# Own rows of the keys first, no zero fills and a new listed order, in a sparse attention with an MLP behind it

## The chip, the cores and the metric

One core of a Trainium2 chip runs the kernel. The metric is the device time of one execution in microseconds; the figure shown is the median of three runs. The profile is of one such execution, and its span runs from the first to the last instruction. The engines are TensorE (PE, with PEld for its weight loads), VectorE (DVE), ScalarE (ACT), GpSimd (POOL) and SyncE (SP). In this kernel POOL issues all loads from DRAM and SP all stores but one.

## The reference

Block-sparse attention for 4 batches, 8 heads, 768 positions and 64 dimensions, then an MLP of 512 to 2048 to 512 over the 3072 tokens. Each query sees the keys at a distance under 16, and the 24 blocks of 32 keys by the block's maximum (with log 32 added to the score) and the block's mean value.

```python
k_sum = k.reshape(B, H, nb, block, D).max(axis=3)
v_sum = v.reshape(B, H, nb, block, D).mean(axis=3)
scores_l = scale * np.matmul(q, k.transpose(0, 1, 3, 2))
mask_l = np.abs(pos[:, None] - pos[None, :]) < window
scores_s = scale * np.einsum('bhsd,bhnd->bhsn', q, k_sum)
scores_s = scores_s + np.log(block)
scores_l_m = np.where(mask_l, scores_l, -1000000000.0)
scores_all = np.concatenate([scores_l_m, scores_s], axis=-1)
...
a = np.exp(scores_all)
a = a / (np.sum(a, axis=-1, keepdims=True) + 1e-09)
v_all = np.concatenate([v, v_sum], axis=2)
return np.matmul(a, v_all).astype(np.float32)
...
h = x @ w_in
relu6 = np.clip(h + 3.0, 0.0, 6.0)
g = h * relu6 / 6.0
return (g @ w_out).astype(np.float32)
```

## The kernel before

**Tiling.** The 768 positions of a batch are cut into 12 tiles of 64 keys. A tile's window has 96 key rows: 64 own and 32 of a neighbour. Behind them stand 24 rows for the blocks, 120 rows in all (`KEYS`). The 64 queries of tile t are shifted by 16 against its keys, so that the window covers every key at a distance under 16. `kaug[p]` holds the keys of head pair p by tile, as columns; `vaug[b % 2]` holds the values with the 120 rows on partitions, and with a column of ones whose product is the softmax's denominator. Before the change a window is previous 32 rows, then own 64: own rows lie in rows 32 to 95, and queries are shifted down by 16. The first tile wraps around to the last rows of the batch.

**Steps of one batch.** Keys are transposed (`k_step` for batch 0, by products with the unit matrix `ident`; `turn` for the others, by VectorE), the block maximum is taken (kmax) and spread over the tiles. Values land by a strided load, which turns f32 into bf16, into the own rows; the neighbour's 32 rows are copied from the own rows of another tile (`halo`, batches 0 and 1) or loaded again (`load_ahead`, batches 2 and 3). Block sums of V are products with the indicator `ind` (`vsum_first`, `vsum`), spread over tiles by copies. Scores go to PSUM, ScalarE takes the exp, VectorE masks, values are a product with `vaug`, VectorE normalizes, and the result is transposed into `x`. A batch has two halves of 384 positions; each half is a tile s of the MLP (8 in all). `f1` multiplies by `w_in` (16 items of 128 features, 4 products of 384 columns each), with relu on ScalarE and the gate on VectorE; `f2` multiplies by `w_out` (three row groups ts, four parts of four products), copies to SBUF and stores.

**Order.** Every step registers operations with a key. The string `ORDER` lists all keys in the order in which they are issued; each engine works its own operations strictly in that order, and `:A` or `:D` picks ScalarE or VectorE for a copy. Keys: `c` constants; `K`, `Q`, `V`, `H` loads of keys, queries, values and neighbour values; `Q0w2` a wide load of queries; `I` and `O` loads of `w_in` and `w_out`; `k`, `q`, `w` transposes of K and Q; `h` halos; `u` block sums; `s` scores; `v` values; `F` and `G` the two MLP products. So `K00` loads pair 0 of batch 0 (192 KB), `K02` pairs 2 and 3 (384 KB); `c.1` makes `ident` and `c.2` the band of the mask, both on POOL. `u0` sums V of pairs 0 and 1, `v410` and `v411` are the values of batch 0's second half.

A token `~n`, `-n`, `_n` or `=n` places **fill products** on the tile `idle`, whose results nobody reads: n of 512, n of 128, n of 64 columns, or one of 64 n columns (`keep`, line 774).

PSUM has three buffers h, one o and two pairs S. Each F item takes an h (some early ones may take an S) and frees it with its gate.

**Zero fills.** `c.8` to `c.15` (`empty`, line 280) write zeros to the 32 neighbour rows of `vaug` ahead of the halos, so that the sums over 96 rows read defined data; five stand on ScalarE and three on VectorE.

**The end.** The last G group (s = 7, ts = 1) is done in column pieces of 256, 128 and 128, each with its own copy; the middle 128 are copied and stored by ScalarE (line 698), the others are stored by SP (lines 694 and 695, two DMAs where rows wrap).

Of the kernel before, what the change touches and what calls it, by code (L numbers as in the profile page):

```python
# [15 lines left out]
D = 64  # L16
# [17 lines left out]
s020.1 v01.3 v00.3 V03.0 u1.0 u1.3:A h030.0:D s030.0 k3.4 ~2 s030.1 u1.4:D v01.4 h031.0:D Q0w0.0 Q0w1.0 v01.5:D Q0w2.0 =1 q3.0
q3.1:D q2.0 u1.1:A u1.2:D s020.2 v02.0 v02.1 v02.2 s021.0 v02.3 s030.2 v03.0 v03.1 q2.1:A v03.2 s011.0 v03.3 v00.4 v00.5:D
v02.4 s021.1 s011.1 s021.2 v03.4 v03.5:D s011.2 v02.5:A s031.0 s031.1 s001.0 s031.2 I2.0 F0x3.0 F0x3.1 F0x3.2 F0x3.3 F0x3.4
F0x3.5 I4.0 F0x6.0 F0x6.1 F0x6.2 F0x4.0 F0x4.1 F0x4.2 F0x4.3 v411.0 v411.1 F0x5.0 F0x4.4 F0x4.5 v411.2 s001.1 I8.0 u0.2:A
s001.2 F0x8.0 F0x8.1 F0x8.2 F0x5.1 I0.0 F0x5.2 F0x11.0 F0x1.0 F0x11.1 F0x11.2 F0x1.1 F0x1.2 F0x1.3 F0x1.4 F0x1.5 v410.0 v410.1
F0x7.0 F0x7.1 F0x7.2 v410.2 F0x10.0 F0x10.1 I12.0 F0x13.0 F0x13.1 F0x15.0 F0x15.1 F0x13.2 F0x10.2 v411.3 v411.4:D v410.3
v410.4:A F0x15.2 F0x14.0 F0x14.1 F0x14.2 F0x9.0 F0x9.1 F0x9.2 F0x0.0 F0x0.1 F0x2.0 F0x2.1 K13.0 K10.0 c.12:A F0x0.2 K12.0 K11.0  # L40
w10.0 Q1w1.0 F1x14.0 F1x14.1 F1x14.2 F1x4.0 F1x4.1 F1x4.2 F1x2.0 F1x2.1 F1x2.2 w10.1:D F0x2.2 F0x2.3 F0x2.4 F0x12.0 F0x12.1
F0x12.2 F1x8.0 F1x8.1 F1x8.2 F1x1.0 F1x1.1 F1x1.2 F0x0.3 F0x0.4 F0x0.5 F0x2.5 F1x9.0 F1x9.1 F1x9.2 F1x5.0 F1x5.1 F1x5.2 F1x15.0
F1x15.1 w11.0 w11.2 F1x15.2 w11.3:D Q1w4.0 Q1w2.0 Q1w0.0 w10.2 w10.3:D q6.0 q6.1:A q7.0 q7.1:A F1x7.0 F1x7.1 w11.1:A F1x7.2
F1x12.0 F1x12.1 F1x12.2 O0.0 G02x0.0 Q1w5.0 Q1w3.0 q4.0 q4.1:A q5.0 q5.1:A F1x6.0 F1x6.1 F1x6.2 O1.0 G02x0.1 s100.0 s100.1
s100.3 F1x3.0 w12.0 F1x11.0 F1x11.1 w13.0 w13.2 F1x3.1 F1x11.2 w12.2 w12.1:D O2.0 G02x0.2 s101.0 s101.1 O3.0 F1x10.0 G02x0.3
G02x0.4:A w13.3:D w13.1:A s101.3 F1x0.0 G00x0.0 G00x0.1 w12.3:D s100.2 s101.2 s100.4 V10.0 h100.0:D F1x10.1 h110.0:A F1x10.2
F1x3.2 s110.0 s110.1 s110.2 s101.4 s110.3 G00x0.2 G00x0.3 G00x0.4:A V12.0 u4.0 h130.0:D h120.0:A F1x0.1 u4.1:D u4.2:A u4.4:D
u4.3:D u4.5:D G02x0.5 G01x0.0 G01x0.1 G01x0.2 s110.4 F1x0.2 h111.0:A v100.0 v100.1 v100.2 h121.0:A v101.0 v101.1 v101.2 G01x0.3
G01x0.4:A K20.0 K21.0 K22.0 K30.0 K23.0 w21.0 F1x13.0 F1x13.1 F1x13.2 v100.3 v100.4:A w20.0 w21.3 G12x0.0 w21.2:A v101.3
v101.4:A V22.0 H2.0 h101.0:A w20.3 G12x0.1 G12x0.2 F2x2.0 F2x2.1 F2x11.0 F2x2.2 F2x11.1 F2x11.2 s111.0 w23.0 s111.3 F2x1.0  # L50
F2x1.1 F2x1.2 F2x3.0 F2x3.1 F2x3.2 F2x15.0 F2x15.1 F2x15.2 Q22.0 w23.3 G12x0.3 s111.1 G12x0.4:A F2x5.0 F2x5.1 h131.0:A F2x5.2
F2x6.0 G10x0.0 s111.2 w22.0 w22.3 s111.4 w23.4:A V20.0 H2.1:A K33.0 F2x13.0 F2x13.1 F2x13.2 G10x0.1 F2x6.1 F2x0.0 F2x0.1 F2x0.2
u5.0 u5.1:A u5.5:A F2x6.2 v110.0 v111.0 v111.1 v111.2 Q30.0 F2x4.0 F2x4.1 F2x4.2 Q21.0 Q23.0 Q20.0 w22.4:A F2x10.0 F2x10.1
# [24 lines left out]
F6x3.2 G52x0.3 G52x0.4:D F6x5.0 F6x5.1 F6x11.2 F6x2.0 F6x2.1 F6x5.2 F6x2.2 G51x0.0 F6x13.0 F6x13.1 F6x6.0 F6x15.0 G51x0.1
v311.6 F6x6.1 F6x6.2 F6x15.1 v311.5 v311.4 F7x5.0 F6x15.2 F6x13.2 F7x5.1 F7x5.2 F7x13.0 F7x9.0 F7x13.1 F7x13.2 F7x9.1 F7x9.2
G51x0.2 F7x12.0 F7x12.1 F7x12.2 F7x10.0 F7x10.1 F7x10.2 F7x1.0 G51x0.3 F7x1.1 F7x1.2 G51x0.4:A F7x3.0 G40x0.5 F7x6.0 F7x6.1  # L80
F7x6.2 G51x0.5 F7x8.0 F7x8.1 F7x8.2 G62x0.0 F7x4.0 F7x4.1 F7x4.2 F7x3.1 F7x3.2 F7x2.0 G62x0.1 F7x15.0 F7x2.1 F7x2.2 F7x15.1
F7x15.2 F7x0.0 G62x0.2 F7x0.1 G62x0.3 F7x7.0 F7x7.1 F7x0.2 G71x0.0 G62x0.4:D G62x0.5 F7x7.2 F7x11.0 F7x11.1 G61x0.0 F7x11.2
F7x14.0 G71x0.1 G71x0.2 G71x256.0 G61x0.1 F7x14.1 F7x14.2 G71x0.3 G71x0.4:A G72x0.0 G72x0.1 G71x0.5 G41x0.5 G70x0.0 G61x0.2
# [79 lines left out]
def kernel(  # L163
# [80 lines left out]
    def low(x):  # L244

        return (1 - x) * HQ
# [17 lines left out]
    def spread_mask():  # L264
        nc.vector.tensor_copy(mask[:], band[:].unsqueeze(1).to_broadcast([WIN, NQ, QB]))
        nc.vector.memset(mask[0:BLK, 0, PAD:QB], 0.0)
        for lo in (BLK, 2 * BLK):
            nc.vector.memset(mask[lo:lo + BLK, 0, 0:PAD], 0.0)
# [48 lines left out]
    def load_wide(b, u):  # L317
# [492 lines left out]
```

## Time and profile before

| what | us |
|---|---|
| median of 3 runs (216.97 to 217.23) | 217.14 |
| span of the profiled execution | 214.9 |
| TensorE busy | 208.8 |
| VectorE busy | 162.7 |
| ScalarE busy | 135.9 |
| F products (line 667, 500 on h) | 91.1 |
| G products (line 684, 336 on o) | 81.7 |
| fill products (line 778), 80 of them | 9.5 |

Busy time counts the union of an engine's instructions, and ends of products are modelled. A row of a timeline gives start, duration, engine, line, operation, output and input, and, in brackets, how long the engine was idle before and what ended that. A row of a group gives count, busy time, mean in ns and idle time before. A row of DMA issues gives queue, count, size and the time from issue to landing. The DMA engines are nearly always busy in the first 91 us, since loads run far ahead of their use.

### The profile page before, as it was taken

How to read it: one execution, taken by the hardware profiler on the slowest of the kernel's cores; microseconds unless marked ns; L12 is line 12 of the kernel's file. 1: busy time of each engine (PE TensorE's matmuls, PEld its weight loads, DVE VectorE, ACT ScalarE, POOL GpSimd, SP SyncE). 2: the span in 40 equal slices, each digit the busy share in tenths (PEclk: the TensorE clock that was granted, in tenths of full speed). 3: DMA queues.
4: the chain of work that ended last, by engine and by line, in shares of the span. 5: the costliest groups of instructions: out<-in, count | busy, mean ns of one | idle time of the engine just before them, and what ended most of it. 6: DMA issues, size and time to landing. Idle time of an engine off the chain costs nothing.

```text
span 214.9 us, 6125 instructions
## 1 busy us (share of the span) xinstructions
PE 208.8 (97%) x2564; PEld 119.7 (56%) x2564; DVE 162.7 (76%) x318; ACT 135.9 (63%) x264; POOL 49.5 (23%) x66
## 2 busy tenths in 40 slices
PE   7998999999999999999999999999999999999994
PEld 7566656555555565565555555555555555564443
DVE  6987999999899999898899889887865555550021
ACT  3987878887898988756578696566346355520110
POOL 7977358906643244000000000000000000000000
PEclk9999999999999999999999999999999999999999
DMA  5999999999999999930334234113314400113123
GB/s 75 159 155 189 203 188 170 190 203 162 206 160 187 181 135 151 108 146 11 38 37 143 28 37 110 49 21 39 70 19 81 78 0 3 49 49 122 52 80 139
DMA packets 91724, 22.68 MB, mean 106 GB/s; under 512 B 82224, under 2 KB 88752, under 8 KB 91696
## 3 DMA queue, kind: packets, MB, share of 16 engines
q0 software_dynamic: 62288, 14.41, 72.7%
q1 hardware_dynamic: 29264, 7.80, 15.4%
q8 instruction: 20, 0.33, 0.6%
q10 hardware_dynamic: 144, 0.07, 0.1%
q14 instruction: 8, 0.07, 0.1%
HBM read 28.82 MB, written 6.29 MB: 163 GB/s over the span
## 4 chain that ended last, share of the span: by engine, by line
PE 86%; POOL 5%; DMA 4%; DVE 1%; ACT 1%; issue 1%; POOLq 0%
PE h L667 38%; PE o L684 33%; PE h L684 5%; DMA qwide<-in_q_dram 4%; PE S L624 3%; PE S L513 3%; POOL vaug L344 2%; PE S L554 1%; ACT vaug L242 1%; POOL first L306 1%; PE S L637 1%; POOL qwide L326 1%; PE S L440 1%; PE S L667 1%; POOL first L313 1%; PE h L582 1%
## 5 line engine op out<-in xcount | busy, mean ns | idle before, releaser
L667 PE MATMUL h<-x,win 128*128 128x384 bf16 x500 | 91.1, 326 | 0.3 <-DVE g L672 0.3
L671 ACT ACTIVATE r<-h 128x384 f32<-128x384 f32 x125 | 58.7, 492 | 38.8 <-PE h L667 36.8
L672 DVE SCALAR_TENSOR_TENSOR g<-r,h 128x384 bf16<-128x384 f32 x125 | 65.7, 546 | 22.7 <-ACT r L671 20.1
L684 PE MATMUL o<-wout,g 128*128 128x512 bf16 x336 | 81.7, 379 | 0.0
L667 PEld LDWEIGHTS <-win 128*128 128x128 bf16 x512 | 48.7, 98 | 35.9 <-issue 0.5
L684 PEld LDWEIGHTS <-g 128*128 128x128 bf16 x416 | 38.7, 98 | 37.4 <-issue 0.3
L521 ACT ACTIVATE at<-S 120x768 bf16<-120x768 f32 x24 | 18.6, 811 | 5.5 <-PE S L513 5.4
L242 ACT COPY ot<-o 128x512 f32<-128x512 f32 x17 | 10.0, 586 | 15.4 <-PE o L684 14.2
L522 DVE TENSOR_TENSOR at<-at,mask 96x768 bf16<-96x768 bf16 x24 | 12.6, 549 | 2.0 <-ACT at L521 1.6
L606 DVE TENSOR_TENSOR xn<-S,rc 128x768 bf16<-128x768 f32 x14 | 13.3, 950 | 0.3
L242 DVE COPY ot<-h 128x512 f32<-128x512 f32 (+1 forms) x3 | 1.6, 555 | 14.3 <-PE h L684 14.3
L344 POOL DMA_DIRECT2D vaug<-in_v_dram x10 | 11.8, 1191 | 0.4 <-DMA first<-in_k_dram 0.2
L684 PE MATMUL h<-wout,g 128*128 128x128 bf16 (+2 forms) x80 | 11.4, 294 | 0.0
L468 DVE TENSOR_REDUCE red<-kaug 128x24 bf16<-128x768 bf16 x12 | 11.2, 942 | 0.1
L242 ACT COPY vaug<-vaug 32x640 bf16<-32x640 bf16 (+3 forms) x17 | 8.9, 574 | 0.8 <-DMA vaug<-in_v_dram 0.5
L242 ACT COPY vaug<-vs 24x1536 bf16<-24x1536 bf16 x6 | 8.8, 1468 | 0.6 <-DVE vs L242 0.5
L456 DVE STREAM_TRANSPOSE kaug<-kraw 128x768 bf16<-128x768 bf16 x8 | 8.1, 1020 | 0.3 <-PE S L513 0.3
L778 PE MATMUL o<-idle 128*128 128x64 bf16 (+2 forms) x70 | 7.0, 278 | 1.1 <-DVE idle L288 1.1
L334 POOL DMA_DIRECT2D kraw<-in_k_dram x8 | 5.9, 737 | 8.9 <-DVE kaug L456 7.3
L513 PEld LDWEIGHTS <-kaug 32*128 32x128 bf16 x576 | 5.3, 92 | 4.4 <-issue 3.6
L643 DVE STREAM_TRANSPOSE y<-xn 128x768 bf16<-128x768 bf16 x8 | 7.6, 964 | 0.2
L624 PEld LDWEIGHTS <-at 120*64 120x64 bf16 x336 | 6.2, 111 | 2.6 <-issue 1.5
(107 smaller groups left out, 183.6 us busy)
## 6 DMA issues: line engine op xcount, KB each, us to landing
out_dram<-ot SPq DMA_DIRECT2D x19, 256.0 KB, 2.3
vaug<-in_v_dram POOLq DMA_DIRECT2D x6, 384.0 KB, 13.1
wout<-in_moe_w_out_dram POOLq DMA_DIRECT2D x4, 512.0 KB, 9.9
win<-in_moe_w_in_dram POOLq DMA_DIRECT2D x3, 512.0 KB, 10.8
kraw<-in_k_dram POOLq DMA_DIRECT2D x8, 192.0 KB, 12.9
x<-y SPq DMA_DIRECT2D x64, 24.0 KB, 2.0
first<-in_k_dram POOLq DMA_DIRECT2D x6, 192.0 KB, 12.3
first<-in_q_dram POOLq DMA_DIRECT2D x6, 192.0 KB, 12.3
```

Of the source, the lines that this page charges most:

```text
L242: {"ACT": nc.scalar.copy, "DVE": nc.vector.tensor_copy, "POOL": nc.gpsimd.tensor_copy}[eng](o, i)
L344: op("POOL", "dma128", lambda: nc.gpsimd.dma_start(out=o[BLK:WIN, a:z, 0:D], in_=rows[:, a:z]), w=[("v", b % 2, c) for c in range(lo, hi)] ...
L468: op("DVE", "max", lambda: nc.vector.tensor_reduce(red.slot[:], w[:, :, BLK:WIN].rearrange("p t (n c) -> p t n c", n=2), axis=AX.X, op=ALU ...
L513: nc.tensor.matmul(X[g // 2].slot[:, g % 2, i * QB:(i + 1) * QB], kaug[2 * u + m][rows, t], qT[rows, 2 * u + m, t * QB:(t + 1) * QB], star ...
L521: op("ACT", "exp", lambda a=a, e=e: nc.scalar.activation(a, X[e].slot[0:KEYS, :, 0:HALF], AF.Exp, scale=scl), r=[X[e]], w=[("at", p, half)])
L522: op("DVE", "masking", lambda m=m: nc.vector.tensor_tensor(m, m, mask[:, low(half):low(half) + HQ].unsqueeze(1).to_broadcast([WIN, 2, HQ, ...
L606: nc.vector.tensor_tensor(o, src[..., 0:D], r.unsqueeze(len(r.shape)).to_broadcast(list(o.shape)), op=ALU.mult)
L624: nc.tensor.matmul(X.slot[64 * c:64 * c + 64, i, m:m + D + 1], a[:, t * QB:(t + 1) * QB], vaug[b % 2][0:KEYS, h, t, 0:D + 1], start=True, ...
L667: nc.tensor.matmul(bank(h)[:, 0:HALF], w_in_sb[:, kt, cols], xt[s].slot[:, kt], start=(kt == 0), stop=(kt == NP - 1))
L671: op("ACT", "relu", lambda: nc.scalar.activation(r.slot[:], bank(h)[:, 0:HALF], AF.Relu, bias=0.5, scale=1.0 / 6.0), r=[h], w=[r])
L672: op("DVE", "gate", lambda: nc.vector.scalar_tensor_tensor(gt[s].slot[:, ft], r.slot[:], 1.0, bank(h)[:, 0:HALF], op0=ALU.min, op1=ALU.mul ...
L684: nc.tensor.matmul(o.slot[:, a:z], gt[s].slot[:, ft, ts * 128:(ts + 1) * 128], w_out_sb[:, ft, a:z], start=(ft == 0), stop=(ft == NFT - 1))
```

## The change

The window becomes own 64 rows, then the next 32. Own rows lie in rows 0 to 63 and the neighbour's in 64 to 95; queries are shifted up by 16; the last tile wraps, no longer the first. `low` is turned around, so that half 0 is the first half of the positions. The sums read the 64 own rows alone, `ind` has 64 rows, and the zero fills go. The store in two pieces moves from ts = 0 to ts = 2 of the second half.

The whole `ORDER` is new. In its beginning there are two new groups of fill products ahead of the first two `k` steps, `~7 _33` and `~6 =8`, then `~2 =7` and `~1`; there are none behind `u0.0`. In all 51 fill products with 11,264 columns stand where 80 with 15,296 stood. At its end the last piece is `G71x256`, the one that ScalarE copies and stores.

```diff
 ORDER = """
-c.0 K00.0 c.7 c.17 c.6 c.8:A K01.0 c.10:D c.5 c.1 _40 -15 k0.0 k0.2:A c.18 ~1 =2 k1.0 K02.0 ~12 =3 k2.0 k3.0 c.15:D c.2 c.3
-s000.0 k0.3:A c.13:D c.4 c.11:A k1.1 Q00.0 q0.0 k1.4 k0.1 c.20 k1.2:A Q01.0 ~2 =5 q1.0 k0.4 k1.3:D c.9:A c.14:A c.19 k2.3:A
...
-G70x0.4:D G70x0.5 G60x0.0 G60x0.1 G60x0.2 G72x0.4:D G72x0.5 G60x0.3 G71x256.1 G71x256.2 G60x0.4:D G60x0.5 G71x256.3 G71x256.4
-G71x384.0 G71x384.1 G71x384.2 G71x384.3 G71x384.4:D G71x384.5
+c.0 c.10 c.8 c.7 c.6 K02.0 Q01.0 c.12 c.5 K00.0 c.1 Q00.0 K01.0 c.11 c.9 V00.0 V01.0 ~7 _33 k2.0 c.2 ~6 =8 k0.0 k2.2:A V03.0
+k2.1 c.3 k2.3:A k0.1 V02.0 q1.0 k0.4 k0.2:A q1.2:A s000.0 Q0w2.0 Q0w1.0 q1.1:A q0.0 Q0w0.0 I2.0 k3.0 k1.0 k0.3:A q0.1:D q0.2:D
+k1.1 I4.0 k1.4 k3.3:A k2.4 s010.0 k1.2:A k3.1 I8.0 s000.1 s000.2 h011.0:D ~2 =7 s010.1 s010.2 k3.4 ~1 u0.0 s030.0 k3.2:A
+h010.0:D h000.0:D h030.0:D u0.3:A c.4 s020.0 I0.0 u0.1:A s020.1 I12.0 s030.1 v01.0 k1.3:A K12.0 s020.2 v00.0 v00.1 h020.0:D
+v00.2 v00.3 v01.1 v01.2 s030.2 u1.0 u1.1:A u1.3:D v02.0 v03.0 v03.1 v02.1 v01.3 h001.0:A u0.2:D v03.2 K13.0 v02.2 K10.0 v00.4
+u1.2:D v01.4 K11.0 Q1w3.0 v02.3 q3.0 h021.0:A v03.3 q3.1:D q2.0 s021.0 v02.4 v00.5:D O0.0 v03.4 q2.1:D v02.5:D v01.5:A s011.0
+F0x3.0 F0x3.1 h031.0:A s021.1 s031.0 F0x3.2 s011.1 v03.5:D F0x3.3 s001.0 F0x6.0 s031.1 s001.1 Q1w4.0 u1.4:D s021.2 s011.2
...
+G71x384.2 G71x384.3 G60x0.4:A G70x0.1 G72x0.4:A G71x384.4:D G71x384.5 G70x0.2 G60x0.5 G71x0.0 G72x0.5 G70x0.3 G71x0.1 G71x256.0
+G71x0.2 G71x256.1 G71x0.3 G71x0.4:A G71x256.2 G50x0.5 G70x0.4:D G71x256.3 G70x0.5 G71x256.4 G71x0.5
...
-    ind = sb([WIN, NQ, 32], BF16, "ind")
+    ind = sb([QB, NQ, 32], BF16, "ind")
...
-        return (1 - x) * HQ
+        return x * HQ
...
-    def empty(eng, i, c):
...
-    for i in range(2):
-        for c in range(NP):
-            op(EITHER, "empty", lambda eng, i=i, c=c: empty(eng, i, c), r=["idle"], w=[("vh", i, c)])
...
-        op("POOL", "dma128", lambda: nc.gpsimd.dma_start(out=o[BLK:WIN, a:z, 0:D], in_=rows[:, a:z]),
+        op("POOL", "dma128", lambda: nc.gpsimd.dma_start(out=o[0:QB, a:z, 0:D], in_=rows[:, a:z]),
...
-            copy(eng, o[0:BLK, hs, a:z, 0:D], o[QB:WIN, hs, a - 1:z - 1, 0:D])
+            copy(eng, o[QB:WIN, hs, a:z, 0:D], o[0:BLK, hs, a + 1:z + 1, 0:D])
...
-                    nc.tensor.matmul(T.slot[lo:lo + BLK, 0:2 * D], ind[:, t], vaug[0][0:WIN, 2 * c:2 * c + 2, t, 0:D],
+                    nc.tensor.matmul(T.slot[lo:lo + BLK, 0:2 * D], ind[:, t], vaug[0][0:QB, 2 * c:2 * c + 2, t, 0:D],
...
-            b, row = s // 2, 128 * ((s % 2 * 3 + ts + 3) % 6) - PAD
-            n = max(-row, 0)
+            b, row = s // 2, 128 * (s % 2 * 3 + ts) + PAD
+            n = max(row + 128 - S, 0)
```

More of the change, by code (lines that the diff above doesn't have):

```diff
@@ L34 @@
[L34 to L41, printed above, removed]
@@ L352, in load_ahead @@
         o = t[:].rearrange("p h t d -> p (h t) d")
[L353 to L355 removed]
+        op("POOL", "dma128", lambda: nc.gpsimd.dma_start(out=o[QB:WIN, 0:n - 1, 0:D], in_=rows[0:BLK, 1:n]),
+           w=[("vh", i), ("vh0", i)] + [("vh", i, c, x) for c in range(NP) for x in range(2)], size=32 * 95)
+        op(EITHER, "round", lambda eng: copy(eng, t[QB:WIN, :, NQ - 1, 0:D], t[0:BLK, :, 0, 0:D]),
            r=[("v", i, c) for c in range(NP)], w=[("vh", i), ("vh0", i)])
@@ L442, in tr @@
                         nc.tensor.transpose(bank(T).bitcast(BF16)[:, at_:at_ + 128], src[:, p * 128:(p + 1) * 128], ident[:])
-        op("PE", "qwtr4" if b else "qwtr", tr, r=[("qw", b, (1 - half) * m + u) for u in range(m)] + ["ident"], w=[T])
-        lo = low(half) * QB
+        op("PE", "qwtr4" if b else "qwtr", tr, r=[("qw", b, half * m * (b > 0) + u) for u in range(m)] + ["ident"], w=[T])
+        lo = low(half) * QB + PAD
         op(EITHER, "qwcopy", lambda eng: copy(
```

169 lines of the change are left out of this document (82 added, 87 removed).

## The prediction

> **What bounds the kernel now.** I read the page first, then the busy time by stretches of 10 us, then the start of TensorE's timeline, because the page shows TensorE busy almost everywhere.
>
> ```profile
> span 214.9 us, 6125 instructions
> 20.00:30.00 10.00, 9.52 (x192) 6.56 (x193) 8.59 (x20) 8.20 (x14) 4.06 (x5) 1.00 1.36 201
> 70.00:80.00 10.00, 10.00 (x144) 5.95 (x143) 9.22 (x17) 8.78 (x19) 3.19 (x4) 1.00 1.65 165
> ```
>
> In the rows of stretches the columns are span, PE, PEld, DVE, ACT, POOL, granted clock, DMA. From 70 us on TensorE has no gap, and none of the products that it does there is removed. So time can be won only where TensorE waits or does fill products (on the tile `idle`, results never read), which is the first 24 us, and in the tail behind the last product.
>
> ```profile
> 1.13 3.71 PE L778 MATMUL o<-idle 128*128 128x64 bf16 x55 [1.13 <-DVE idle L288]
> 4.82 0.53 PE L392 MATMUL h<-ident,first 96*64 96x96 bf16 x16
> 6.45 2.85 PE L778 MATMUL o<-idle 128*128 128x512 bf16 x13
> 14.28 0.85 PE L536 MATMUL o<-vaug,ind 96*32 96x128 bf16 x24
> 20.31 0.73 PE L442 MATMUL h<-ident,qwide 128*128 128x128 bf16 x10 [0.81 <-DMA qwide<-in_q_dram]
> 24.17 2.12 PE L667 MATMUL h<-x,win 128*128 128x384 bf16 x12
> 32.57 0.83 PE L637 MATMUL S<-ident,xn 128*128 128x128 bf16 x12
> ```
>
> Until the first F product at 24.17 TensorE waits or fills for about 11 us: 4.82 at the start, 2.85 from 6.45, 0.81 at 20.31, and some 3 in the shorter pieces of the same timeline. Behind 24.17 it runs almost without a hole. What the change is worth is therefore how much earlier the same early work is finished. That work is fed by one queue, POOL's, and prepared by VectorE and ScalarE.
>
> ```profile
> 1.36 1.42 POOL L306 DMA_DIRECT2D first<-in_k_dram  x2 [0.84 <-POOLq L794]
> 2.76 0.22 POOL L250 MEMSET ident<- 128x128 bf16 x1
> 3.31 0.73 POOL L306 DMA_DIRECT2D first<-in_k_dram  x1
> 6.07 3.77 POOL L344 DMA_DIRECT2D vaug<-in_v_dram  x4
> GB/s 0 0 0 0 0 23 61 195 197 211 135 74 137 186 197 149 162 191 166 181 186 146 154 156 156 155 157 155 156 156 151 153 153 154 156 169 214 184 200 208
> first<-in_k_dram POOLq DMA_DIRECT2D x1, 192.0 KB, 3.4
> first<-in_k_dram POOLq DMA_DIRECT2D x1, 384.0 KB, 5.5
> vaug<-in_v_dram POOLq DMA_DIRECT2D x2, 192.0 KB, 7.1
> ```
>
> The GB/s row is the DMA view of 0 to 20 us in slices of 0.5 us. Issued at 1.36, K00 lands 3.4 later, at 4.76. K02, issued at 3.31, lands at 8.8. V01, the second of the four issues from 6.07, lands at about 14.1, just before the first sums at 14.28. Between 5.0 and 6.5 us the stream sags to 135, 74 and 137 GB/s: the making of `ident` stands on POOL between K01 and K02.
>
> **The change part by part.**
>
> *Order of loads.* K02, Q01 and K00 now go first and only then `ident`, so the sag should go. Against 200 GB/s it loses (65 + 126 + 63) x 0.5 / 200 = 0.6 us. Everything behind it lands about 0.6 earlier with equal bytes ahead: V01 at 13.5, and the last wide Q, whose landing ended the wait before 20.31, at 19.7. But the first load is twice as big. A 192 KB piece takes 1.0 to 1.3 in the stream, so K02 lands at about 5.9, and the first K product moves from 4.82 to there. Then Q01 7.2, K00 8.3, Q00 9.5, K01 10.6.
>
> *Fills.* The first row of them has 40 x 64 + 15 x 128 = 4480 columns in 3.71 us, 0.83 ns a column. The 13 of 512 in 2.85 us are 0.43 ns a column. The new 7 x 512 + 33 x 64 = 5696 columns from 1.13 on end between 3.6 and 5.9 by these two, before K02. The next seven (1.5 us) stand in a wait of some 1.9, from 6.4 to 8.3; three before the second score product (0.6) in a wait for VectorE; one (0.2) in that for V01. I price all at nothing, since waits for data cover them. Without that cover they would cost at most their own 2.3.
>
> *Zero fills.* They go from both engines.
>
> ```profile
> L285 ACT ACTIVATE vaug<-idle 32x768 f32<-32x768 bf16 x5 | 4.1, 836 | 0.0
> L283 DVE MEMSET vaug<- 32x768 f32 x3 | 2.1, 698 | 0.4 <-issue 0.2
> 6.63 0.96 DVE L403 TENSOR_REDUCE red<-h 128x24 bf16<-128x768 bf16 x1
> ```
>
> That is 6.2 us of engine time, nearly all of it in waits for K. VectorE's last one does hold up the first kmax, at 6.63, but in the new order VectorE waits for K02 there anyway. So nothing by itself; if the loads came a microsecond earlier than I think it would be worth up to 0.7. The sums read 64 rows in place of 96 with the same 128 columns, so I price them as before; the bounds are 0.85 a group either way and a third of it (0.3 a group) less. Copies, turns, scores and values keep counts and shapes, only partitions and block numbers change.
>
> *VectorE's chain.* From K01's landing on VectorE sets the pace. The durations:
>
> ```profile
> L408 DVE COPY kaug<-red 128x288 bf16<-128x288 bf16 x4 | 1.2, 302 | 0.1
> 15.18 0.35 DVE L242 COPY vaug<-vaug 32x768 bf16<-32x768 bf16 x1
> L606 DVE TENSOR_TENSOR xn<-h,rc 128x384 bf16<-128x384 f32 x4 | 2.1, 555 | 0.1
> L599 DVE RECIPROCAL rc<-h 128x6 f32<-128x6 f32 x4 | 0.7, 186 | 0.1
> 20.75 0.56 DVE L242 COPY qT<-h 128x768 bf16<-128x768 bf16 x1 [0.87 <-PE h L442]
> L496 ACT ACTIVATE at<-S 120x768 bf16<-120x768 f32 x8 | 6.3, 810 | 0.3
> L672 DVE SCALAR_TENSOR_TENSOR g<-r,h 128x384 bf16<-128x384 f32 x125 | 65.7, 546 | 22.7 <-ACT r L671 20.1
> ```
>
> K01 at 10.6 gives k1's products by 11.1. In listed order VectorE then does two kmax (1.9), three spreads (0.9), five halos, one in two pieces (1.85), and the mask (0.55, an estimate: a copy of a halo's 768 elements and two small memsets): 5.2, to 16.3. TensorE does u0 at 13.5 (14.28 before) and ends the first two pairs' values at 16.7. VectorE goes on with four normalizations at 0.56 + 0.19 (3.0), four small copies of block sums and two of x at about a halo's 0.35 (2.1) and two q copies (1.1): 6.2, to 22.5. TensorE waits about 0.3 for the wide Q, 0.8 for the first q copy and 0.2 for the second. The last scores and the first F products follow, and the second F item starts at about 23.7. Before, it started behind four products of the row at 24.17, at 24.85: 1.15 earlier.
>
> What is late next is the gate. The four exps of the second half (3.2) and their masks stand before the first relu and gate in the list. Walking on at one exp in 0.81 and one gate in 0.55, the first gate ends at 26.1, and three buffers come late by 0.1 to 0.3. The product of line 637 at 32.57, with eleven F items ahead of it, compares with 31.7 in the new order: 0.9 earlier. I take 1.0.
>
> *Tail.* The last product was a quarter copied by VectorE and stored by SP; the last is now the quarter whose copy and store are both ScalarE's.
>
> ```profile
> 211.11 0.27 ACT L698 COPY ot<-h 128x128 f32<-128x128 f32 x1 [5.26 <-PE h L684]
> 211.96 0.29 DVE L242 COPY ot<-h 128x128 f32<-128x128 f32 x1 [0.82 <-PE h L684]
> out_dram<-ot ACTq DMA_DIRECT2D x1, 64.0 KB, 2.1
> out_dram<-ot SPq DMA_DIRECT2D x1, 64.0 KB, 1.6
> ```
>
> The copies are equal; the store is 0 (if 2.1 came from company on the queues) to 0.5 longer, and I take 0.2. SP's last stores, G70 and a half of G71, wait for copies that end before ScalarE's last. The store in two pieces moves from G70 to G72, earlier in the list: nothing.
>
> **Sum** on the profiled execution: 214.9 - 1.0 + 0.2 = 214.1. The median shown, 217.14, lies 2.24 above the span, which I leave alone: **216.3**.
>
> **The rivals.**
>
> 1. *The early chain is tighter than my walk.* If the three waits behind the wide Q's landing (1.3) go and K00 lands where the fills end (0.4), 216.3 - 1.7 = 214.6. For it: the new list has no fill behind u0. Against it: VectorE's 6.2 behind 16.3 has no slack.
>
> 2. *The gain is given back in batch 1.* Its values wait for block sums that ScalarE spreads.
>
> ```profile
> 59.56 1.48 ACT vaug L242
> 46.91 0.86 PE o L684 x4
> ```
>
> In the new list ScalarE has an exp (0.8), an output copy and a halo (some 0.6 each) and such a spread (1.48) before the first values of batch 1, 3.5 in all; behind the sums stand one F item (0.65) and two G groups (0.86 each) as cover, 2.4 and the sums' own 0.84. That alone is a wait of 0.3. If V of batch 1 or the exp is 0.5 to 0.7 late as well, the whole gain is eaten: 216.9 to 217.2. Against it: ScalarE is not full there.
>
> 3. *VectorE falls behind in the first F items: slower.* From 22.5 on it has four masks (2.2), two normalizations of 128x768 (2.3), six gates (3.3) and a spread before TensorE's tenth item gets a buffer: 8.2, against 7.4 of products. I count 0.25 of waits. Only three h buffers stand between; if each of four items waits for one gate of 0.55 more, that is 2.2: 216.3 + 2.0 = 218.3. From 0.8 more than I count it decides the sign. For it: VectorE is at 8.59 of 10 in this stretch already. Against: before, the same work left TensorE only 0.5 of waits.
>
> 4. *V loads at half rate: slower.* V's own rows now land in partitions 0 to 63 in place of 32 to 95. Three loads behind one another answer this, by their issues and the time from issue to landing:
>
> ```profile
> 51.18 0.71 POOL L334 DMA_DIRECT2D first<-in_k_dram  x1
> 51.88 1.34 POOL L344 DMA_DIRECT2D vaug<-in_v_dram  x1
> 53.21 1.40 POOL L353 DMA_DIRECT2D vaug<-in_v_dram  x1
> first<-in_k_dram POOLq DMA_DIRECT2D x1, 192.0 KB, 9.8
> vaug<-in_v_dram POOLq DMA_DIRECT2D x1, 384.0 KB, 12.0
> vaug<-in_v_dram POOLq DMA_DIRECT2D x1, 380.0 KB, 13.7
> ```
>
> They landed at 61.0, 63.9 and 66.9: V into 64 partitions took 2.9 for 384 KB, and the neighbour rows, into partitions 0 to 31 alone, 3.0 for 380 KB. So the lower partitions alone were no slower. At half rate V00 and V01 would come 2.2 later, and 216.3 + 2.2 = 218.5; from 0.8 on it decides. [...]
>
> **How the numbers follow.** My forecast 0.45 (216.3, its own range 215.5 to 216.9), rival 1 0.15, rival 2 0.20, rival 3 0.13, rival 4 0.07. A measurement of this kernel can tell about 0.2% (0.43 us) from no change. Faster holds the forecast and rival 1: 0.60; same is rival 2: 0.20; slower is 3 and 4: 0.20. The range takes rival 1 and rival 2 whole, the tail's bounds and the mild part of rival 3: 214.6 to 217.8.
>
> **What would show it.** In the changed profile the first K product near 5.9, the GB/s row without its sag, u0 near 13.5 and the second F item near 23.7 show the early steps right; line 637's first group near 31.7 shows the gates in time; a last store of 1.6 to 2.1 behind ScalarE's copy shows the tail. I am wrong if K00 lands behind 9, if TensorE waits for gates over 1 us between 24 and 33, or if a new wait of over 0.5 stands between 45 and 90 us.

## The result and the profile after

The changed kernel takes 220.74 us (median of 4 runs, 220.30 to 221.25), the kernel before 217.19 on the same chip (4 runs, 216.97 to 217.29). The ratio is 1.0174, with a 95% interval of 1.0152 to 1.0196: slower by 1.7%, where 216.3 was forecast and 217.8 was the upper end of the range. Of some kernels below (e3, e4, e8, e9) the runs fall into two groups several us apart, the slower one mostly at a lower mean clock; medians are over all runs of a kernel, ratios leave out most of the slower group.

The profiled execution is 4.6 us longer than that of before (219.5 against 214.9). Three lines of its page:

```profile
span 219.5 us, 6029 instructions
PEclk9999589999999999999999999999999999999999
q8 instruction: 20, 0.33, 0.6%
```

PEclk has a hole in slices 5 and 6 (22 to 33 us). The kernel before has none in 20 to 30 us, where the prediction's row shows 1.00. The same stretch after, and seconds of it (columns: stretch, its length, PE, PEld, DVE, ACT, POOL, granted clock, DMA share, GB/s):

```profile
20.00:30.00 10.00, 8.18 (x116) 4.70 (x116) 7.71 (x19) 6.43 (x12) 4.73 (x7) 0.66 1.39 199
22.00:23.00 1.00, 0.69 (x18) 0.60 (x17) 0.78 (x3) 0.97 (x2) 0.11 (x1) 0.75 1.25 209
24.00:25.00 1.00, 1.00 (x15) 0.47 (x14) 0.94 (x4) 0.62 (x2) 0.33 (x1) 0.50 1.44 202
28.00:29.00 1.00, 1.00 (x4) 0.45 (x3) 0.95 (x3) 0.62 (x2) 0.52 (x1) 0.50 1.71 182
29.00:30.00 1.00, 1.00 (x36) 0.56 (x36) 0.41 (x1) 0.45 (x1) 0.09 (x1) 0.84 1.81 180
```

TensorE looks full from 23 to 29 us, but at half clock: F products of 128x384 come every 0.33 to 0.4 us, where before they came every 0.18 (12 in 2.12). Over the ten us the mean clock is 0.66, so (1 - 0.66) x 10 = 3.4 us of full speed are missing.

Waits of TensorE after (time in all, times, longest), then its timeline:

```profile
PE S L503 <- issue: 1.7, 1, 1.7
PE h L580 <- DVE xn L596: 1.5, 1, 1.5
PE o L382 <- ACT qT L241: 1.0, 1, 1.0
PE S L480 <- ACT kaug L241: 0.4, 1, 0.4
```

```profile
6.17 0.53 PE L382 MATMUL h<-ident,first 96*64 96x96 bf16 x16 [0.34 <-DMA first<-in_k_dram]
14.29 0.84 PE L526 MATMUL h<-vaug,ind 64*32 64x128 bf16 x24
19.68 0.34 PE L580 MATMUL h<-ident,xn 128*128 128x128 bf16 x3
21.52 0.33 PE L580 MATMUL h<-ident,xn 128*128 128x128 bf16 x3 [1.50 <-DVE xn L596]
26.83 2.68 PE L657 MATMUL h<-x,win 128*128 128x384 bf16 x8
35.87 0.50 PE L627 MATMUL S<-ident,xn 128*128 128x128 bf16 x6
49.34 0.53 PE L503 MATMUL S<-qT,kaug 32*128 32x64 bf16 x46
51.52 0.20 PE L503 MATMUL S<-qT,kaug 32*128 32x64 bf16 x2 [1.65 <-issue]
```

Two stops stand out: 1.50 before 21.52, and 1.65 before 51.52, in the middle of 48 equal score products whose data were all there. The second F item starts at 26.83 (24.85 before). Line 627 comes in two halves after; with eleven F items ahead, and 0.33 taken off for the half that is already done, it stands at 35.54, 3.0 later than the 32.57 of before. Then 1.65 for the second stop, and 0.15 in the tail: 4.8, where the spans differ by 4.6.

The first stop is put down to VectorE's `xn`. VectorE's timeline contradicts it:

```profile
18.15 0.56 DVE L596 TENSOR_TENSOR xn<-h,rc 128x384 bf16<-128x384 f32 x1
19.16 0.56 DVE L596 TENSOR_TENSOR xn<-h,rc 128x384 bf16<-128x384 f32 x1
20.92 0.56 DVE L596 TENSOR_TENSOR xn<-o,rc 128x384 bf16<-128x384 f32 x1
```

The groups at 19.68 and 21.52 (`v00.4`, `v01.4`) read the first two, complete at 19.72 at the latest. The one that ends at 21.48 serves a later product (23.27). It only happened to end as the stop did.

What did arrive 2.5 us before the stop ended is a packet of the instruction queue q8 (at 19.08): 0.33 MB in 20 packets, 16 KB each. TensorE's program has 5070 rows (2535 products, each of them two rows, a weight load and a product; the page counts 2535 weight loads); 20 packets of 256 rows hold 5120, so I read a packet as 256 rows of 64 bytes, an estimate from these numbers. The kernel before fits if some rows are there from the start: 2564 weight loads, so 5128 rows, in 20 packets too. Counted from the program's start, `v01.4` begins at row 701. The second stop is ahead of row 1467, which is 766 rows, by this reading three packets less two rows, further on.

### The profile page after: what moved, and what is told of

Its sections match the earlier page's. It is cut to its first block, busy times and chain, and to the rows that moved or that the text cites. A ratio compares the mean times of both kernels' runs of the same rounds, so it can differ in the third digit from the quotient of the medians.

```text
span 219.5 us, 6029 instructions
## 1 busy us (share of the span) xinstructions
PE 207.7 (95%) x2508; PEld 118.5 (54%) x2535; DVE 159.6 (73%) x314; ACT 127.3 (58%) x259; POOL 49.1 (22%) x66
## 4 chain that ended last, share of the span: by engine, by line
PE 84%; DMA 4%; POOL 3%; DVE 3%; issue 2%; ACT 2%; ACTq 0%; POOLq 0%
PE h L657 38%; PE o L674 31%; PE h L674 5%; DMA vaug<-in_v_dram 4%; PE S L503 3%; PE S L614 2%; DVE xn L596 2%; POOL vaug L334 1%; ACT vaug L241 1%; POOL first L295 1%; PE S L657 1%; PE S L627 1%; PE S L480 1%; PE S L430 1%; PE S L544 1%
## 5 line engine op out<-in xcount | busy, mean ns | idle before, releaser
L657 PE MATMUL h<-x,win 128*128 128x384 bf16 x500 | 94.4, 331 | 0.0
L661 ACT ACTIVATE r<-h 128x384 f32<-128x384 f32 x125 | 59.9, 493 | 52.6 <-PE h L657 50.5
L674 PE MATMUL o<-wout,g 128*128 128x512 bf16 x310 | 78.0, 379 | 1.9 <-issue 0.8
L657 PEld LDWEIGHTS <-win 128*128 128x128 bf16 x512 | 48.9, 99 | 36.7 <-issue 1.0
L241 ACT COPY ot<-o 128x512 f32<-128x512 f32 x15 | 8.8, 586 | 16.1 <-PE o L674 16.1
L674 PE MATMUL h<-wout,g 128*128 128x512 bf16 (+2 forms) x79 | 10.7, 293 | 0.1
L241 DVE COPY ot<-h 128x128 f32<-128x128 f32 (+1 forms) x2 | 1.0, 492 | 11.5 <-PE h L674 7.8
L503 PE MATMUL S<-qT,kaug 32*128 32x64 bf16 x576 | 6.8, 190 | 1.7 <-issue 1.7
L241 ACT COPY kaug<-h 128x576 bf16<-128x576 bf16 (+3 forms) x12 | 4.2, 434 | 6.4 <-PE h L382 4.7
L768 PE MATMUL o<-idle 128*128 128x64 bf16 (+1 forms) x47 | 6.4, 312 | 1.1 <-DVE idle L279 1.1
L241 ACT COPY kaug<-kaug 128x352 bf16<-128x352 bf16 (+1 forms) x24 | 7.2, 365 | 0.0
## 6 DMA issues: line engine op xcount, KB each, us to landing
first<-in_k_dram POOLq DMA_DIRECT2D x6, 192.0 KB, 13.2
```

The lines of the kernel that those rows point to most:

```text
L241: {"ACT": nc.scalar.copy, "DVE": nc.vector.tensor_copy, "POOL": nc.gpsimd.tensor_copy}[eng](o, i)
L503: nc.tensor.matmul(X[g // 2].slot[:, g % 2, i * QB:(i + 1) * QB], kaug[2 * u + m][rows, t], qT[rows, 2 * u + m, PAD + t * QB:PAD + (t + 1) ...
L657: nc.tensor.matmul(bank(h)[:, 0:HALF], w_in_sb[:, kt, cols], xt[s].slot[:, kt], start=(kt == 0), stop=(kt == NP - 1))
L661: op("ACT", "relu", lambda: nc.scalar.activation(r.slot[:], bank(h)[:, 0:HALF], AF.Relu, bias=0.5, scale=1.0 / 6.0), r=[h], w=[r])
L674: nc.tensor.matmul(o.slot[:, a:z], gt[s].slot[:, ft, ts * 128:(ts + 1) * 128], w_out_sb[:, ft, a:z], start=(ft == 0), stop=(ft == NFT - 1))
```

## The experiments

| run | us (lowest to highest, runs) | ratio to before (95%) | granted clock, 20 to 30 us |
|---|---|---|---|
| after | 220.74 (220.30 to 221.25, 4) | 1.0174 (1.0152 to 1.0196) | 0.66 |
| e1_fill | 224.19 (223.13 to 226.36, 4) | 1.0365 (1.0320 to 1.0410) | |
| e2_half | 221.59 (220.31 to 222.12, 4) | 1.0219 (1.0186 to 1.0253) | |
| e3_layout | 217.96 (216.39 to 223.25, 12) | 1.0031 (1.0008 to 1.0055) | |
| e4_rows | 218.00 (216.95 to 221.09, 10) | 1.0035 (1.0002 to 1.0068) | 0.83 |
| e5_rows_fill | 218.23 (216.45 to 219.68, 10) | 1.0056 (1.0021 to 1.0092) | 0.66 |
| e6_more_rows | 220.31 (220.14 to 220.48, 2) | 1.0132 (1.0078 to 1.0186) | |
| e7_fills | 217.03 (216.72 to 218.55, 12) | 1.0022 (1.0005 to 1.0038) | 1.00 |
| e8_best | 223.97 (220.52 to 225.40, 6) | 1.0241 (1.0184 to 1.0298) | |
| e9_before_less | 218.06 (216.14 to 222.08, 10) | 1.0011 (0.9979 to 1.0044) | 0.50 |
| e10_early_copy | 218.54 (217.86 to 218.94, 8) | 1.0062 (1.0038 to 1.0086) | 1.00 |
| e11_layout_fills | 217.02 (216.51 to 217.47, 12) | 1.0001 (0.9984 to 1.0018) | 1.00 |

The clock is that of the profiled run. The kernel before was run beside each; its medians lie between 216.74 and 217.19.

### Fills where the wait is: e1 and e2

My first theory took the wait before 21.52 at its word and put fills into it, to keep the clock up.

```diff
-u1.2:D v01.4 K11.0
+u1.2:D ~7 v01.4 K11.0
```

e2 has `~3` there.

> The changed kernel with seven fill products of 512 columns (1.5 us at the full rate) ahead of v01.4, where TensorE waited 1.5 us for VectorE. Theory A (the wait of 1.5 us amid small products lets the clock fall to half from 22.8 to 29.2 us): the granted clock stays 1.00 from 20 to 30 us, four F products take 0.65 us again at once, and the time falls by about 3 us, to 217.5 to 218. Theory B (the clock falls for another reason, and VectorE's delay alone makes the loss): the clock stays at 0.5 there and the time is 220.5 within 0.5. If the 1.65 us stall inside s100.0 at 50 us comes from something that differs from run to run, it is gone or elsewhere here.

> The changed kernel with three fill products in the same place, which leaves about 0.85 us of wait, as long as the one of 0.81 that the kernel before had at the full clock. Theory A with a bound on the length of the wait: the clock stays 1.00 and the time is that of the full fill, 217.5 to 218. If any such wait counts in proportion: the clock still falls, for part of the stretch or all of it, 219 to 220.7. Theory B: 220.5 within 0.5.

TensorE's timeline of e1:

```profile
19.82 0.34 PE L580 MATMUL h<-ident,xn 128*128 128x128 bf16 x3
22.12 3.10 PE L768 MATMUL S<-idle 128*128 128x512 bf16 x7 [1.96 <-issue]
50.47 0.47 PE L503 MATMUL S<-qT,kaug 32*128 32x64 bf16 x39
52.63 0.26 PE L503 MATMUL S<-qT,kaug 32*128 32x64 bf16 x9 [1.70 <-issue]
```

The fills read `idle` and need nothing from VectorE, yet they stood too, for 1.96 us, and then ran at half clock (7 in 3.10). Neither expectation held, and VectorE isn't what TensorE waits for there. The second stop moved too: 39 of 48 products now stand ahead of it, 46 after. Seven products fewer, for seven fills more: the same row of the program, 1467. That led to the theory of instruction packets. e2 has the stop in the same place (1.4) and a second phase at 0.53 to 0.62 from 12 to 16 us: slower than expected as well.

### The layout alone: e3 and e11

e3 is the changed code under the `ORDER` of before, tokens renamed where constants and wide loads are numbered differently.

```diff
-c.0 c.10 c.8 c.7 c.6 K02.0 Q01.0 c.12 c.5 K00.0 c.1 Q00.0 K01.0
...
+c.0 K00.0 c.7 c.9 c.6 K01.0 c.5 c.1 _40 -15 k0.0 k0.2:A c.10 ~1 =2 k1.0 K02.0
...
```

> The changed code (own rows first, no zero fills, sums over 64 rows) with the listed order of before, its tokens renamed and the zero fills left out of it. If the new order alone costs the time: 216.7 to 217.2, the clock 1.00 throughout, V landing as before. If the layout costs (V into partitions 0 to 63 at half rate): V00 and V01 2 us later and 218.5 or more.

It came out at 1.0031, and neither stop is there. In its profile the clock fell to 0.50 in 20 to 22 us, behind two waits for V of 0.4 and 0.3; four of its twelve runs took 220.4 to 223.3 us, at a mean clock of 0.967 to 0.984. e11 puts two fills of 512 columns into each of these waits:

```diff
-~2 =5 v00.0 V01.0 u0.0
+~2 =5 v00.0 V01.0 ~2 u0.0
-V03.0 u1.0 u1.3:A
+V03.0 ~2 u1.0 u1.3:A
```

> The old listed order with the new layout (217.96, where the clock fell behind three waits for V of 0.2 to 0.4 us), with two more fill products ahead of u0.0 and two ahead of u1.0. If the layout costs only through the clock: 216.5 to 217.2 and no run above 219. If the layout itself costs: 217.5 or more with the clock at 1.00.

217.02 against 217.00, ratio 1.0001, with a mean clock of 0.998 or more in all twelve runs. Own rows first, sums over 64 rows and no zero fills are together worth nothing that can be measured, either way, once four more fills hold the clock; without these it is the 0.3% of e3. The rest of the 1.7% comes from the new order.

### Rows of the program: e4 and e6

If TensorE stops because row 701 isn't there yet, the stop must stay with the row whatever the row does. By the count of weight loads a wide product takes as many rows as a narrow one, so the number of rows ahead can be changed at nearly the same time. e4 has 29 products fewer (58 rows), e6 has 23 more (46 rows):

```diff
-V01.0 ~7 _33 k2.0
+V01.0 ~11 k2.0
```

```diff
-V01.0 ~7 _33 k2.0
+V01.0 ~4 _59 k2.0
```

> The changed kernel whose first 40 fill products (7 of 512 columns, 33 of 64) are 11 of 512: nearly the same columns (5632 for 5696), but 58 instruction rows of TensorE fewer (a product and its weight load are two rows). Theory C (TensorE's instructions come in blocks of 256 rows by DMA, and a block that is due less than some 5 us behind the one before is waited for: in both runs so far TensorE stopped at row 701 and again at row 1467, whatever stood there): row 701 now falls on v02.4, reached some 5 us behind row 445 in place of 3.9, so the wait of 1.5 us behind v00.4 shrinks to 0.5 or less, the wait at s100.0 moves on by 29 products or goes, the clock stays 1.00 from 20 to 30 us, and the time is 216.5 to 218. Theory A' (v01.4 waits for VectorE's normalization at that place): the wait of 1.5 us stays ahead of v01.4 and the time is 220 to 221.

> The changed kernel with the first fill products as 4 of 512 and 59 of 64 columns: 46 rows more. Theory C: TensorE stops at row 701 again, which now lies among the products of v03.0 to v02.1 (rows 645 to 740), so the wait stands inside those values and none of 1.5 us ahead of v01.4; the second wait comes 23 products earlier than s100.0's 46th. Time 219 to 222. Theory A': the wait stays ahead of v01.4.

e6, TensorE's timeline:

```profile
19.51 0.25 PE L572 MATMUL h<-vf,at 24*64 24x65 bf16 x4
21.97 0.31 PE L572 MATMUL h<-vf,at 24*64 24x65 bf16 x8 [2.22 <-issue]
22.41 0.78 PE L580 MATMUL h<-ident,xn 128*128 128x128 bf16 x6
48.88 0.35 PE L503 MATMUL S<-qT,kaug 32*128 32x64 bf16 x23
49.84 0.37 PE L503 MATMUL S<-qT,kaug 32*128 32x64 bf16 x25 [0.62 <-issue]
```

The first stop now cuts twelve equal products of values in two, ahead of row 701 again; `v01.4` waits for nothing (six products in one row at 22.41). The second stop has moved ahead by 23 products, which is 46 rows. This is the clearest proof: a stop that moves by exactly the 46 rows that were added belongs to the program's supply, not to data. One packet of q8 starts to arrive 2.3 to 2.5 us ahead of the end of the first stop in each of four kernels (at 19.1 in after, 19.8 in e1, 19.4 in e6, 18.7 in e8), and one 2.4 to 2.8 us ahead of the end of the second in after, e1 and e6 (48.9, 49.9 and 47.4).

In e4 neither stop is left:

```profile
19.93 0.51 PE L580 MATMUL h<-ident,xn 128*128 128x128 bf16 x6
20.28 0.83 PE L432 MATMUL S<-ident,qwide 128*128 128x128 bf16 x12
22.70 0.47 PE L480 MATMUL S<-qT,kaug 64*128 64x64 bf16 x12 [1.58 <-DVE qT L241]
26.51 1.47 PE L657 MATMUL h<-x,win 128*128 128x384 bf16 x8
34.34 0.50 PE L627 MATMUL S<-ident,xn 128*128 128x128 bf16 x6
47.81 0.55 PE L503 MATMUL S<-qT,kaug 32*128 32x64 bf16 x48
```

Its ratio is 1.0035, 2.7 us below after by the medians. But TensorE now waits 1.58 for VectorE's copy of q, and the scores at 22.70 start only 0.13 earlier than in after (22.83): by itself the first stop took the place of a wait that was there anyway. Behind it, in after the clock is low until 29.3, in e4 until 26.2; from these scores to the mark of line 627 (34.01 in e4) it is 12.7 us in after and 11.3 in e4. That the stop made the low phase longer isn't shown: e6, with a longer stop, is low for 3.4 us, and e5 below, without one, for 6.8. Behind the mark both run the same list at the full clock, and e4 is some 1.6 us shorter: that is the second stop, whose 48 products are in one row here (47.81).

Why the packet was late in after and not in e4 can be read from the rows ahead of it. From row 445, by my reading the first of the packet before, to row 701 TensorE needed 3.9 us in after (16.1 to the stop at 20.0), 6.0 in e4 and 6.6 in the kernel before. The packet of row 701 starts to arrive 3.0 us (after) to 3.7 us (before) behind row 445, and in after it was of use 2.4 later.

### The clock: e5, e7 and e9

e4 still had 3.4 us of half clock. e7 adds eight wide fills in three waits; e5 has four in another place, ahead of `k1.0`.

```diff
-V01.0 ~7 _33 k2.0
+V01.0 ~11 k2.0
...
-s030.2 u1.0
+s030.2 ~2 u1.0
...
-K10.0 v00.4
+K10.0 ~2 v00.4
...
-q2.0 s021.0
+q2.0 ~4 s021.0
```

> The same with four more fill products in the wait of 1.0 us ahead of k1.0 (10.4 to 11.4 us). If only the blocks of instructions matter: as the run before it, within 0.5 us. If the early waits matter for the clock too: the clock holds at least as well, and the time is equal or up to 1 us shorter where the other one's clock fell.

> The kernel of 58 fewer rows (218.0, its clock down from 22.9 to 26.9 behind a wait of 1.6 us for VectorE) with eight fill products of 512 columns in the sparse stretch: two ahead of u1.0, two ahead of v00.4, four ahead of s021.0. Theory D (the clock falls where TensorE does too little in the last few us, by waits and by small products alike, and fills hold it): the clock stays 1.00 throughout, the F products run at the full rate from the first on, and the time is 1.5 to 2 us under that of 58 fewer rows, 216 to 217. If fills take as much as the clock gives back: 217.5 to 218.5.

The stretches of e7 and then of e5, with the columns as above:

```profile
20.00:30.00 10.00, 9.86 (x176) 6.27 (x176) 9.76 (x24) 7.80 (x17) 4.43 (x6) 1.00 1.37 201
```

```profile
20.00:22.00 2.00, 2.00 (x25) 1.78 (x19) 1.87 (x7) 1.95 (x5) 1.83 (x3) 0.54 1.25 209
22.00:24.00 2.00, 1.22 (x19) 1.01 (x18) 1.70 (x5) 0.99 (x3) 0.38 (x1) 0.50 1.24 204
```

e7 keeps the full clock: 217.03, span 215.0, ratio 1.0022. Its F products come at their old pace and the mark of line 627 is reached soonest:

```profile
23.12 0.35 PE L480 MATMUL S<-qT,kaug 64*128 64x64 bf16 x12
25.55 1.48 PE L657 MATMUL h<-x,win 128*128 128x384 bf16 x8
33.38 0.50 PE L627 MATMUL S<-ident,xn 128*128 128x128 bf16 x6
```

From these scores to the mark it is 9.9 us, 2.8 less than in after. The ratios of e7 and e4 (1.0022 and 1.0035) differ by less than their intervals; what differs beyond doubt is the clock. Its mean is 0.998 or more in all twelve runs of e7, and goes down to 0.976 in the ten of e4. In e5 the clock was at 0.54 in 20 to 22 us already, with no wait over 0.23 from 14.24 to its fall at 20.2; the only long wait of this stretch, 0.78, ended at 22.87. So here no long wait was needed. What the stretch from 16 us on has is many small products: of 64, 65 or 128 columns, until 20 us on 24 to 96 partitions.

If fills hold the clock, the kernel before should lose it without its own. e9 is the kernel before less its last six:

```diff
-s000.2 ~2 =5 v00.0
+s000.2 v00.0
...
-k3.4 ~2 s030.1
+k3.4 s030.1
...
-Q0w2.0 =1 q3.0
+Q0w2.0 q3.0
```

> The kernel before without its six last fill products (two and one ahead of v00.0, two ahead of s030.1, one ahead of q3.0; 1.2 us of fills in waits). Theory D: the clock falls to half for some 3 us between 18 and 28 us, and the time rises by 1 to 3 us. If fills hold nothing here: 217 within 0.5.

Five of its ten runs took 216.1 to 216.8 us at a mean clock of 1.00; the other five took 219.3 to 222.1 at 0.96 to 0.98. The 23 runs of before beside it all took 216.0 to 217.3. The profiled run is one of the long ones:

```profile
16.00:18.00 2.00, 1.91 (x56) 1.68 (x57) 1.82 (x7) 2.00 (x4) 1.36 (x2) 0.73 2.38 158
18.00:20.00 2.00, 1.86 (x24) 0.97 (x18) 1.40 (x4) 1.16 (x5) 2.00 (x4) 0.50 1.47 201
28.00:30.00 2.00, 2.00 (x8) 0.94 (x7) 0.56 (x1) 0.93 (x2) 0.65 (x1) 0.50 1.66 185
```

Half clock from 17 to 30 us, with TensorE busy in 93 to 100% of it. By the ratio, over the shorter runs in the main, e9 equals the kernel before. So the six fills, under 2 us of work that nobody reads, seem to be what keeps this stretch fast in every run. Only the long runs of e9 show it, with none such in the 23 of the kernel before; what makes one run of e9 long and another not isn't shown. The pairs that differ by fills alone, e4 and e7, e3 and e11, point the same way.

### V into partitions 0 to 63: m_v

This kernel does only the four loads of V's own rows of batch 0, four times over, into partitions 32 to 95, 0 to 63, 32 to 95 and 0 to 63, and stores zeros; attention and MLP are left out.

> Only the loads of V of batch 0, four pieces of 192 KB behind one another, four times over with waits between: into partitions 32 to 95, 0 to 63, 32 to 95, 0 to 63. All else is left out and the output is zeros. If the lower 64 partitions are served at a lower rate: the second and fourth group take longer from the first issue to the last landing, by up to twice the transfer. If the placement is no cost: all four within 0.3 us.

```profile
5.72 3.86 POOL L53 DMA_DIRECT2D t<-in_v_dram  x4 [5.27 <-DVE t L49]
14.77 1.76 DVE L51 COPY t<-t 128x6144 bf16<-128x6144 bf16 x1 [1.35 <-DMA t<-in_v_dram]
16.82 3.79 POOL L53 DMA_DIRECT2D t<-in_v_dram  x4 [7.25 <-DVE t L51]
25.82 1.76 DVE L51 COPY t<-t 128x6144 bf16<-128x6144 bf16 x1 [5.29 <-DMA t<-in_v_dram]
27.88 3.76 POOL L53 DMA_DIRECT2D t<-in_v_dram  x4 [7.27 <-DVE t L51]
36.80 1.76 DVE L51 COPY t<-t 128x6144 bf16<-128x6144 bf16 x1 [9.21 <-DMA t<-in_v_dram]
```

From the first issue to the copy that the last landing releases it is 9.05, 9.00 and 8.92 us for the first three groups (the fourth has no such copy). At this load (up to 153 GB/s) partitions 0 to 63 load as fast as 32 to 95.

### Two attempts at a better version: e8 and e10

e8 tried to meet the supply from the other side: 66 more products in the first fills, so that TensorE passes row 445 sooner; that the packet with row 701 then comes sooner too was my estimate, from the 3.0 us between the two in after. It also moves one q copy to ScalarE and an exp ahead of the halos, and has three pairs of fills.

```diff
-V01.0 ~7 _33 k2.0
+V01.0 _106 k2.0
...
-q3.1:D q2.0 s021.0 v02.4
+q3.1:A v03.3 ~2 q2.0 s021.0 s021.1 v02.4
...
```

> The changed kernel with 106 fill products of 64 columns at the start (132 rows more, so that the blocks of TensorE's rows begin near 12.5 and 18 us, each some 5 us of work), fills as in the run above but two in place of four late ones, and the copy of q3.1 on ScalarE with its exp ahead of two halos. Theory C and D together: no wait at a block's first row over 0.5 us, the clock at 1.00, s021.0 about 0.8 us earlier than with fills alone, 215.3 to 216.5. If the reorder only moves the wait: equal to the run above.

```profile
18.54 0.39 PE L526 MATMUL h<-vaug,ind 64*32 64x128 bf16 x7
21.24 1.12 PE L526 MATMUL h<-vaug,ind 64*32 64x128 bf16 x17 [2.31 <-issue]
```

The stop is again ahead of row 701, though row 445 was passed at 13.2 in place of 16.1. I had taken the delay from there to the end of the stop for a constant, 5.4 us as in after; here it is 8.0 (5.7 in e1, 6.5 in e6). The packet starts to arrive at 18.7, 5.5 behind row 445; why is open (below). The second stop (1.3 us) is one packet on by my reading, ahead of row 1723. 223.97 us, where 215.3 to 216.5 was expected.

e10 keeps e7's first fills and e8's moves, with two fills ahead of `s021.0` in place of four.

```diff
-v02.3 q3.0 h021.0:A v03.3 q3.1:D q2.0 s021.0 v02.4
+v02.3 v01.5:A q3.0 q3.1:A v03.3 q2.0 ~2 s021.0 s021.1 v02.4
...
```

> The kernel of 58 fewer rows and eight fills, with the copy of q3.1 on ScalarE, its exp ahead of two halos, and two fills in place of the four ahead of s021.0. If VectorE's late copy is the last bound: s021.0 0.5 to 0.8 us earlier, 216.2 to 216.8. If the block of rows that begins at row 701, now among s021.0's products, lands at about 22.9 us whatever stands ahead of it (in the runs so far it was there 2.3 to 2.6 us behind its packet, at 21.2 to 22.9): s021.0 waits for it and the time stays at 217.0 within 0.3.

The clock stays at 1.00 and `s021.0` starts at 22.79, 0.33 earlier than in e7, but new waits follow, and all is lost again: 218.54, ratio 1.0062, outside both expectations. Two rows of its waits:

```profile
PE S L480 <- ACT at L486: 0.7, 2, 0.5
PE S L614 <- DVE at L488: 0.5, 2, 0.3
```

No version tried is faster than the kernel before.

## Why the prediction was wrong, step by step

**The step that failed** is the pricing of the *Fills*: "I price all at nothing, since waits for data cover them." Their own time was indeed covered. What I didn't price is what fills are to TensorE besides time: each is two rows of its program, however narrow (23 products more in e6 moved the second stop by 46 rows), and the wide ones late in the stretch held its clock (1.00 in 20 to 30 us in e7, 0.83 in e4 without them). The new order has 33 narrow ones at the start and takes away the last ones. I walked TensorE's work at the full clock, and with every row at hand, because the profile of before shows nothing else; no rival had either. A change of the first 40 fills alone (e4, 58 rows fewer) takes the ratio from 1.0174 to 1.0035, and eight wide fills more (e7) give the full clock and 1.0022.

The sum, with what the runs measured, at the mark of line 627 and behind it:

| term | forecast | measured |
|---|---|---|
| early work, full clock, no stops (e7 against before, 33.05 against 32.57) | -1.0 | +0.5 |
| half clock of e4, 3.4 us (34.01 against 33.05) | not priced | +1.0 |
| 3.4 us more at half clock and the first stop (after against e4, 35.54 against 34.01; 0.1 of it by the scores at 22.7) | not priced | +1.5 |
| second stop | not priced | +1.65 |
| tail | +0.2 | +0.15 |
| sum | -0.8 | +4.8, of 4.6 in the spans |

Each term is a difference of two profiled executions, and the length of the half clock differs between executions of one kernel, so the split of the two middle terms is this pair's. The first measured term is e7's with its eight added fills, so it bounds that loss from above; e7's span is only 0.1 over that of before, so some 0.5 comes back behind the mark, which stays open.

**Order of loads: half right.** First K product at 6.17 (forecast 5.9); by issue and landing K00 lands at 8.1 (8.3) and K01 at 10.3 (10.6). But the sag isn't gone, it moved to the front. The DMA view of after, 0 to 20 us in slices of 0.5:

```profile
GB/s 0 0 0 0 0 27 33 55 195 209 209 185 200 205 203 188 197 192 207 150 157 154 153 158 179 150 148 155 157 151 152 146 154 152 167 196 197 202 229 193
```

By 7.0 us 659 KB have come (sum of the slices by 0.5 us), 610 before: 50 KB more, a quarter of a us at 200 GB/s, where I had taken 0.6. And u0 came at 14.29, as before (14.28), not at 13.5: it was TensorE's own chain that was late, which waited 1.0 for ScalarE's q copy and 0.4 for its `kaug`. I had walked VectorE alone.

**Zero fills and sums: right.** e11 shows nothing gained, and a group of 24 sums takes 0.84, as before (0.85).

**VectorE's chain: right in kind, too short.** The wait for the first q copy is 1.58 in e4, where no stop hides it; forecast 0.8. As u0 was 0.8 late, that is nearly the whole difference.

**Gates, and rival 3: right to leave it small.** Between 24 and 49 us TensorE waited for no gate, nor did it in e7, where the clock was full. **Rival 2:** the only wait over 0.5 between 45 and 90 us is the second stop; block sums and values of batch 1 were in time. I had named a new wait there as a sign of error; it came, from another cause. (The sum of that rival was off as well: 0.3 and 0.5 to 0.7 more make 217.1 to 217.3, not 216.9 to 217.2.) **Rival 4** fell with m_v: no run shows a half rate or its 2.2 us; partitions 0 to 63 took 9.00 us there, 32 to 95 took 9.05 and 8.92. Rivals 3 and 4 gave 218.3 and 218.5, on the right side for the wrong reasons.

**Tail: right.** ScalarE copies at 216.41 for 0.27 and its store takes 1.7, within the 1.6 to 2.1 named.

## What to carry to other kernels

In these kernels a product on TensorE cost time, two rows of its program (46 for 23 in e6), and had a share in what held the clock (0.83 in e4, 1.00 in e7 with eight wide fills more); where fills are moved, narrowed or dropped, price all three, and look at the granted clock by stretches before calling a fill free. When TensorE stops ahead of a product whose inputs are long done, compare the end of the named releaser with what the product really reads, count the rows, and look for the instruction queue's packets; moving the suspect by a known number of rows settled it here in one run (e6). A stop mattered less here for its length than for where it lay: 1.65 us amid dense products at 50 us were lost whole, while 1.50 at 20 us stood where TensorE would have waited 1.58 for VectorE anyway.

## What the runs showed of the hardware

**TensorE outran its instructions.** In after, e1, e2, e6 and e8 it stopped at the first row of what I read as a 256-row packet while the loads kept the DMA engines full (over 195 GB/s), for 1.4 to 2.3 us, and again later, by this reading at the first rows of packets too (within two rows), for 0.6 to 1.7 (0.62 before 49.84 in e6, 1.70 before 52.63 in e1).

**The clock fell without a long gap.** It went to 0.50 behind waits of 1.5 us (1.50 in after, 1.58 in e4), and in e5 and e9 with no wait over 0.4 close ahead, in half of e9's runs; the 1.65 us amid dense products at 50 us left it at 1.00 in after. It changed in steps: the clock records in the trace of after have 17.07 us at 1.00, 6.83 at 0.50 and 191.15 at 1.00, which is 5, 2 and 56 times 3.413. In the other kernels the granted clock by stretches of 2 us gives low phases of some 3.4 us (e1, e2 twice, e3, e4, e6), 6.8 (e5 and e8) and 13.6 (e9). In the last 3.41 us before the fall TensorE was busy for 1.86 in after (19.10 to 22.51), but for 3.18 in e5 (16.75 to 20.16); the 3.41 us of after that hold the second stop (49.80 to 53.21) have 1.71 busy and 1.00 behind them. So neither waits nor busy time alone decided it, and the kind of product seems to count.

**Still open.** That the packets were late because they queue among the loads is argued from the times (TensorE passed row 445 between 5.4 and 8.0 us before row 701 was usable, longest in e8, where the loads ran at 132 to 155 GB/s from 12 to 18 us) and wasn't tested alone. The trace of after speaks for it in part: its packets start 2.2 to 5.5 us behind the first row of the packet before up to 70 us, and 0.7 and 0.9 behind it in the quiet stretches at 76 and 103 us (rows counted by weight loads), but also only 1.4 behind it at 88.9, where the loads run again. What exactly lets the clock fall wasn't tested alone, nor why a low phase lasts one step in e4 (3.4 us) and two in after (6.8).
